# Unit 0's first product of the experts' layer in seven block products instead of eight

## The chip, the cores and the metric

The kernel runs on one core of a Trainium2 chip. The metric is device time in microseconds (us) of one execution; the median of several executions is compared. The profiled execution has a time of its own and a span (first to last instruction), and all times inside it are counted from the start of the span. An engine is named as in the profile: PE is TensorE (its weight loads are PEld), DVE is VectorE, ACT is ScalarE, POOL is GpSimd, SP is SyncE, which starts most transfers.

## The reference

Two stages. First attention over 8 batches, 8 heads, 576 positions and 64 features, with a band mask (half of the heads plain, half dilated by 4). Then a mixture of 8 experts over the 4608 rows of 512 features: each row takes an expert, or keeps that of the row before it, and passes through that expert's two layers.

```python
for b in range(B):
    prev_e = -1
    for s in range(S):
        fresh_e = int(np.argmax(logits[b, s]))
        if s == 0 or local_gate[b, s] < 0.5:
            e = fresh_e
        else:
            e = prev_e if prev_e >= 0 else fresh_e
        prev_e = e
        ...
        h = np.maximum(x[b, s] @ w1[e], 0.0)
        out[b, s] = p[e] * (h @ w2[e])
```

Everything is fp32. `w1[e]` is 512 x 1024, `w2[e]` 1024 x 512.

## The kernel before

**Attention** runs over 32 pairs of heads (n = 0 to 31), some 3.4 to 5 us each. In iteration n, TensorE makes the scores of pair n (L328, L334); VectorE masks half of them (L339) and ScalarE takes the exponential of both halves (L341). TensorE multiplies with the values of pair n - 1 (L387), and VectorE divides by the sums (L391, L392). GpSimd copies rows of V between blocks of the same pair (L279). Every second iteration TensorE turns rows of an earlier pair into columns (L408, L412), which ScalarE copies out (L409, L414); SP stores them in DRAM for later gathers.

**Routing** is done in four groups of 1152 rows. Each group is a chain of small steps: logits (L441, copied by L445), `fresh` (turned by L453, then ten small steps on VectorE, L455 to L476), `carry` (L484, L486, L488), `carry_over` (L494, L496 to L499), `carry_in` (L504, L505), `choose` (L510 to L524), `gate` (L532 to L538), `place` (L548, L549, L551), `lanes_of` (L557 to L564), four matrices (L575 twice, L585, L591) and their products (L600, added by L605). The second group ends the *early* routing, from which the tokens of units 0 and 1 are taken (L703 the expert numbers, L728 to L738 the token numbers); the fourth ends the *late* one (L617 and `count`, L620 to L691; L701, L703; L718, L722; L728 to L743), from which all other units come. The steps wait in a list (`waiting`). `gap(SHARE)` takes some of them twice in each iteration of attention, by their costs; afterwards `work_gap` takes one lot at each `yield` of a unit's products, and up to two entries of a second list, `soon`, which holds sums. So the order on TensorE, VectorE, GpSimd and SP is the order in which this code runs; ScalarE's alone is left to a scheduler.

**Units.** A unit is 256 rows of one expert (kinds `plain` and `pair`), or 128, 64 or 32. Its rows are gathered by GpSimd (L855, by `tok` and `pos`), turned by TensorE and copied by ScalarE (`features`, L870, L871). `hidden` makes the 1024 hidden values, `output` the product with the second weights. Units 0 and 1 are early, the rest late. A *pair* unit splits each product of 2 x 2 blocks into seven block products in place of eight (`chain`), with sums of blocks that VectorE makes beforehand: four of the first weights (`sums_left`, L818 to L821, into `sums[0]`), four of the tokens (`sums_right`, L824 to L827, into `xc`), the same again for the second product (`sums[1]`, `hc`). Of the first seven, ScalarE copies the first three out of PSUM (L955), VectorE adds three more (L961) and ScalarE applies the relu (L962, L959). A *plain* unit, and unit 0 is the only one, does all blocks: in `hidden` 32 matmuls 256 wide (L925), with a relu after each eight (L927), in `output` 16 matmuls 512 wide (L1011), scaled by L1015.

**Weights.** SP loads them (L781) into slots: a 2 MB load for each of a unit's two weights, skipped by a condition if the slot already holds the expert. Slot 0's first weights are loaded beforehand for expert 0, in four parts in iterations 11, 14, 17 and 20 (L312).

After the last pair of heads come the turning of unit 0's rows, that of the last attention rows, the logits of the last group, and then `run_hidden(0, [])`, `run_output(0, ...)`, `run_hidden(1, ...)`, `output(1)`; in the middle of the last, `feed` asks for the late units' weights and tokens. Unit 2's rows are turned (L870) before the last block product of unit 1's output.

Of the kernel before, what the change touches and what calls it, by code (L numbers as in the profile page):

```python
# [14 lines left out]
Act = mybir.ActivationFunctionType  # L15
# [7 lines left out]
P = 128  # L23
# [3 lines left out]
DK, FK = D // P, F // P  # L27
# [10 lines left out]
NPB = B * NP  # L38
# [179 lines left out]
def whole(ctx, tc, exact, bad, qk, v, wgl, w1, w2, con, adm, msk, qmk, out, cst, wg, ones, warm):  # L218
    nc = tc.nc
# [31 lines left out]
    def bank(shape, name):  # L251
        return banks.tile(shape, F32, name=name, tag="bank")
# [498 lines left out]
    for k in range(n_pairs):  # L751
        i = k // 2 + k % 2 * (n_pairs // 2)
        units.append(dict(kind="pair", col=2 * i, slot=k % 2, late=True))
        while len(others) > min(n_others, max(n_others * (n_pairs - 1 - k) // (n_pairs - 2), k < n_pairs - 1)):
            kind, col = others.pop(0)
# [3 lines left out]
    def of_unit(u, what, j=0, rows=P):  # L759
        return tiles[what, units[u]["late"]][:rows, units[u]["col"] + j:units[u]["col"] + j + 1]  # L760
# [6 lines left out]
    def weights(u, second):  # L767

        i = units[u]["slot"]
        loads.add((u, second))  # L770
        if not second:
            units[u]["held"] = holds.get(i)
            holds[i] = nc.values_load(of_unit(u, "experts", rows=1), engines=[ET.SP], min_val=0, max_val=E - 1,
                                      skip_runtime_bounds_check_because="clamped to the experts")
            units[u]["expert"] = holds[i]
        e, held = units[u]["expert"], units[u]["held"]
        w, s, pattern = (w2, raw2, "p m f -> p (m f)") if second else (w1, raw1, "p m k f -> p (m k f)")
        if second and not units[u]["late"] and isinstance(held, int):
            held = None
        more = {} if held is None else dict(cond=e != held, cond_hint=False)  # L780
        nc.sync.dma_start(out=s[i].rearrange(pattern), in_=w[bass.ds(e, 1)].rearrange("o p x -> (o p) x"), **more)  # L781
# [5 lines left out]
    def gap(add=None):  # L787
        if add is not None:
            credit[0] = min(credit[0] + add, add)
        alone = False  # L790
        while waiting and not alone and (add is None or credit[0] >= 0):
            f, cost, _ = waiting.pop(0)
            credit[0] -= cost
            if f:
                f()
            alone = add is None or not waiting or waiting[0][2]
# [7 lines left out]
    def now(push):  # L804
        for f in push:
            f()
# [22 lines left out]
    def sums_of_weights(u, second):  # L829

        i = units[u]["slot"]
        assert (u, second) in loads
        if second:
            return sums_right(sums[1], *(quarter(raw2[i], k, j, True) for k in range(2) for j in range(2)))
        return sums_left(sums[0], *(quarter(raw1[i], f, k, False) for f in range(2) for k in range(2)))
# [3 lines left out]
    def tiles_of(u):  # L839
        return 2 if units[u]["kind"] in ("pair", "plain") else 1  # L840

    def rows_in(u):
        return dict(half=ROW, few=FEW).get(units[u]["kind"], P)
# [18 lines left out]
    def features(u):  # L862
        kind = units[u]["kind"]
        rows = rows_in(u)
        xe[u] = mw.tile([P, DK, 2 * P], F32, name="xe")
        for j in range(tiles_of(u)):
            x = xg.pop((u, j)).rearrange("p g f -> p (g f)")
            tp = bank([P, DK, P], "tp")
            for kk in range(DK):
                nc.tensor.transpose(tp[:, kk, :rows], x[:rows, kk * P:(kk + 1) * P], ident[:rows, :rows])  # L870
            nc.scalar.copy(xe[u][:, :, j * P:j * P + rows], tp[:, :, :rows])  # L871
        if kind == "pair":
            xc[u] = mw.tile([P, 4, DK // 2, P], F32, name="xc", bufs=1)
            return sums_right(xc[u], *(xe[u][:, 2 * k:2 * k + 2, j * P:(j + 1) * P]
                                       for k in range(2) for j in range(2)))
        return []
# [27 lines left out]
    def hidden(u):  # L904
        i, kind = units[u]["slot"], units[u]["kind"]
        ht[u] = h = stage.tile([P, FK, 2 * P], F32, name="h", bufs=2)
        w, x = raw1[i], xe[u]
        if kind in ("half", "few"):
            rows = rows_in(u)
            parts = P // rows  # L910
            t = bank([P, F // parts], "hp")
            for kk in range(DK):
                for v in range(parts):
                    nc.tensor.matmul(t[v * rows:(v + 1) * rows], lhsT=x[:, kk, :rows],
                                     rhs=w[:, v * FK // parts:(v + 1) * FK // parts, kk], start=(kk == 0),
                                     stop=(kk == DK - 1), tile_position=(0, v * rows), skip_group_check=True)
                yield True
            nc.scalar.activation(h[:, 0:4 // parts].rearrange("p m t -> p (m t)"), t, Act.Relu)
            return
        if kind == "plain":  # L920
            for m in range(FK):
                if m % 2 == 0:
                    t = bank([P, 2, 2 * P], "hp")
                for kk in range(DK):
                    nc.tensor.matmul(t[:, m % 2], lhsT=w[:, m, kk], rhs=x[:, kk], start=(kk == 0), stop=(kk == DK - 1))  # L925
                if m % 2:
                    nc.scalar.activation(h[:, m - 1:m + 1], t, Act.Relu)  # L927
                yield True
            return
        if kind == "full":  # L930
            for m in range(FK):
                if m % (FK // 2) == 0:
                    t = bank([P, FK // 2, P], "hp")
                to = t[:, m % (FK // 2)]
                for kk in range(DK):
                    nc.tensor.matmul(to, lhsT=w[:, m, kk], rhs=x[:, kk, :P], start=(kk == 0), stop=(kk == DK - 1))
                if m % (FK // 2) == FK // 2 - 1:
                    v = m * 2 // FK
                    nc.scalar.activation(h[:, v * FK // 2:(v + 1) * FK // 2, :P],
                                         t, Act.Relu)  # L940
                yield True
            return
        xyz = [bank([P, FK // 2, P], "hp") for _ in range(3)]

        def at(k):
            return h[:, k // 2 * FK // 2:(k // 2 + 1) * FK // 2, k % 2 * P:(k % 2 + 1) * P]

        def product(to, a, b, first):
            for m in range(FK // 2):
                for kk in range(DK // 2):  # L950
                    nc.tensor.matmul(to[:, m], lhsT=a[:, m, kk], rhs=b[:, kk], start=first and m == 0 and kk == 0,  # L951
                                     stop=(kk == DK // 2 - 1), skip_group_check=True)

        def keep(k, of):
            nc.scalar.copy(at((0, 1, 3)[k]), of)  # L955

        def finish(k, of):
            if k == 2:
                nc.scalar.activation(at(2), of, Act.Relu)  # L959
            else:  # L960
                nc.vector.tensor_tensor(at(k), of, at(k), op=Alu.add)  # L961
                nc.scalar.activation(at(k), at(k), Act.Relu)  # L962

        yield from chain((lambda i_, k: quarter(w, i_, k, False), lambda s: sums[0][:, s]),
                         (lambda k, j: x[:, 2 * k:2 * k + 2, j * P:(j + 1) * P], lambda s: xc[u][:, s]),
                         *xyz, product, keep, finish)
        units[u]["sums"] = sums_left(hc, at(0), at(2), at(1), at(3))
# [86 lines left out]
                         *xyz, product, keep, finish)  # L1054


    pause, rows = (None, 0, True), []

    def route(g, slow):
        steps = [(logits, 0, True), (fresh, 3.0, True), (carry, 1.0, True), (carry_over, 0.5, True), (carry_in, 0.5, True),  # L1060
# [30 lines left out]

    def early_weights():
        weights(0, False)

    def late_tokens():
        tokens(True)
        gather(FIRST)

    for n in range(NPB + 2):
        if n < NPB:  # L1100
            (scores_exact if exact else scores)(n)
        for k in range(NPB)[n + 1 if n else 0:n + 2]:
            share(k)
        gap(SHARE)
        if 1 <= n <= NPB:
            values(n - 1)
        if n == NPB + 1:
            assert len(rows) <= 4
            now(features(0))
        if n >= 3 and n % 2 == 1:  # L1110
            turn((n - 3) // 2)
            if (n - 3) // 2 % (2 * GB) == 2 * GB - 1:
                route((n - 3) // 2 // (2 * GB), n == NPB + 1)
        gap(SHARE)
        if n + 3 < NPB:
            load(n + 3)
        if n >= 3 and n % 2 == 1:
            store((n - 3) // 2)
        if n in (11, 14, 17, 20):
            load_first(0, (n - 11) // 3)  # L1120
        if n == NPB + 1:
            weights(0, True)
            weights(1, False)
        if rows:
            if n <= NPB:
                paced(n - 1)
            rows.pop(0)()
# [161 lines left out]
```

## Time and profile before

| | us |
|---|---|
| three executions | 666.64, 667.72, 669.94 |
| their median | 667.72 |
| profiled execution | 663.76 |
| its span | 661.8 |
| PE busy in the span | 646.6 |
| DVE busy in the span | 372.5 |
| L925: TensorE busy, records | 15.1, 64 |
| L925: first start, last start | 152.3, 169.6 |

The granted TensorE clock was 1.00 throughout. A line of groups gives the kernel's line, engine, operation, what is written and read, the shape, how many; behind the bar the busy time in us and the mean ns of one; behind the next the time for which its engine was idle just before them, and what ended that. In a timeline a line begins with start and length in us, and the brackets give the idle time before it and what ended it. Neighbouring fp32 matmuls overlap in the records, so distances between starts tell more than lengths.

### The profile page before, as it was taken

The numbers are of one execution on the slowest core, as the hardware profiler recorded it, in microseconds if no ns is written. First come the engines' busy times: TensorE is split into PE (matmuls) and PEld (weight loads), VectorE is DVE, ScalarE is ACT, GpSimd is POOL, SyncE is SP. The second block draws the span as 40 slices with busy tenths as digits, with TensorE's granted clock in tenths as the row PEclk, the third lists the DMA queues.
The fourth block names the chain that finished last, engine by engine and source line by source line (L and its number), as shares of the span: only waits on it lengthen the run. The fifth ranks groups of instructions, "written<-read, shape, count | busy, mean of one in ns | idle before, by whom it ended". The sixth has DMA issues, their size and how long they took to land. (4 is left out here: it accounts for less than half of the span.)

```text
span 661.8 us, 15170 instructions
## 1 busy us (share of the span) xinstructions
PE 646.6 (98%) x6402; PEld 568.2 (86%) x6402; DVE 372.5 (56%) x755; ACT 188.7 (29%) x348; POOL 188.1 (28%) x169
## 2 busy tenths in 40 slices
PE   8999999999999999999999999999999999999996
PEld 6988888888588999999599989998899989899893
DVE  3558578683596595372537382727464536547441
ACT  3544343442112331222122222231222232223210
POOL 3322222242115420322552153223144113051011
PEclk9999999999999999999999999999999999999999
DMA  8999899749205398574533456541045451454001
GB/s 313 325 297 322 280 283 319 247 124 354 88 33 190 129 418 314 187 280 169 226 132 141 154 203 223 229 164 49 16 177 215 179 219 59 155 193 148 1 32 50
DMA packets 29356, 126.31 MB, mean 191 GB/s; under 512 B 4349, under 2 KB 13789, under 8 KB 25312
## 3 DMA queue, kind: packets, MB, share of 16 engines
q1 hardware_dynamic: 22480, 106.05, 44.4%
q0 software_dynamic: 6800, 19.21, 8.5%
q8 instruction: 52, 0.85, 0.5%
q14 instruction: 24, 0.20, 0.1%
HBM read 142.02 MB, written 19.20 MB: 244 GB/s over the span
## 5 line engine op out<-in xcount | busy, mean ns | idle before, releaser
L979 POOL DMA_INDIRECT out_dram<-y,tok x36 | 55.0, 1527 | 292.3 <-DVE y L1048 124.5
L951 PE MATMUL hp<-xc,sum 128*128 128x128 f32 x720 | 85.6, 275 | 0.4 <-DVE sum L818 0.4
L951 PEld LDWEIGHTS hp<-xc,sum 128*128 128x128 f32 x720 | 82.8, 192 | 0.8 <-PE hp L951 0.5
L1033 PE MATMUL yp<-sum,hc 128*128 128x256 f32 x360 | 82.6, 379 | 0.0
L961 DVE TENSOR_TENSOR h<-hp,h 128x512 f32<-128x512 f32 x45 | 30.9, 690 | 90.8 <-PE hp L951 90.1
L1033 PEld LDWEIGHTS yp<-sum,hc 128*128 128x128 f32 x360 | 68.3, 190 | 9.4
L1048 DVE SCALAR_TENSOR_TENSOR y<-yp,gate,y 128x256 f32<-128x256 f32 x45 | 21.7, 482 | 75.1 <-issue 48.1
L279 POOL COPY vt<-vt 32x1040 f32<-32x1040 f32 x32 | 34.0, 1065 | 94.2 <-DMA vt<-in_v_dram 63.0
L951 PE MATMUL hp<-xe,raw 128*128 128x128 f32 x480 | 58.8, 276 | 0.0
L951 PEld LDWEIGHTS hp<-xe,raw 128*128 128x128 f32 x480 | 56.6, 192 | 1.8 <-issue 1.5
L1033 PE MATMUL yp<-raw,h 128*128 128x256 f32 x240 | 57.0, 380 | 0.0
L334 PE MATMUL two<-kq 64*96 64x64 f32 x1152 | 54.5, 244 | 0.2 <-issue 0.2
L334 PEld LDWEIGHTS two<-kq 64*96 64x96 f32 x1152 | 53.7, 162 | 0.3 <-issue 0.3
L855 POOL DMA_INDIRECT xg<-xd,tok x40 | 45.5, 1138 | 27.3 <-PE hp L951 15.0
L1033 PEld LDWEIGHTS yp<-raw,h 128*128 128x128 f32 x240 | 44.4, 190 | 5.5
L955 ACT COPY h<-hp 128x512 f32<-128x512 f32 x45 | 26.4, 586 | 79.3 <-PE hp L951 75.3
L962 ACT ACTIVATE h<-h 128x512 f32<-128x512 f32 x45 | 28.3, 630 | 67.2 <-DVE h L961 67.2
L855 POOL DMA_INDIRECT xg<-xd,pos x40 | 44.1, 1102 | 11.8 <-issue 10.8
L339 DVE SCALAR_TENSOR_TENSOR pr<-two,mk 96x512 f32<-96x512 f32 x32 | 21.9, 685 | 43.8 <-ACT pr L341 32.3
L387 PE MATMUL pv<-vt,pr 96*64 96x65 f32 x1280 | 44.7, 224 | 1.0 <-POOL vt L279 1.0
L387 PEld LDWEIGHTS pv<-vt,pr 96*64 96x64 f32 x1280 | 40.2, 138 | 3.7 <-POOL vt L279 1.2
L1041 ACT ACTIVATE y<-yp,gate 128x256 f32<-128x256 f32 x45 | 21.2, 474 | 55.5 <-PE yp L1033 48.8
(223 smaller groups left out, 1004.6 us busy)
## 6 DMA issues: line engine op xcount, KB each, us to landing
raw<-in_w_dram SPq DMA_DIRECT2D x48, 2048.0 KB
kq<-in_qk_dram SPq DMA_DIRECT2D x32, 592.0 KB
vt<-in_v_dram SPq DMA_DIRECT2D x32, 292.5 KB
xd<-x SPq DMA_DIRECT2D x16, 512.0 KB
raw<-in_w_dram SPq DMA_DIRECT2D x4, 512.0 KB
xd<-x SPq DMA_DIRECT2D x16, 64.0 KB
xg<-xd,tok POOLq DMA_INDIRECT x40, 3.2
xg<-xd,pos POOLq DMA_INDIRECT x40, 3.4
```

The lines of the kernel that those rows point to most:

```text
L279: nc.gpsimd.tensor_copy(vt[:WIN, :, 1:], vt[QB:, :, :NB - 1])
L334: nc.tensor.matmul(sc[:KW, u, k * QB:(k + 1) * QB], lhsT=kt[h, i * QB:i * QB + KW], rhs=qt[h, i * QB:(i + 1) * QB], start=bool(late), stop ...
L339: nc.vector.scalar_tensor_tensor(pr, sc[:KW, :, :w], -CEIL, mk[:, kind].unsqueeze(1).to_broadcast([KW, 2, w]), Alu.max, Alu.min)
L387: nc.tensor.matmul(pv[h * QB:(h + 1) * QB, k - a, u], lhsT=pr[i][:, u], rhs=vt[:, u, i], start=True, stop=True, tile_position=(0, h * QB), ...
L855: nc.gpsimd.indirect_dma_start(out=x[:rows, g], out_offset=None, in_=xd[g] if units[u]["late"] else xd[g][:EARLY * GS], in_offset=bass.Ind ...
L951: nc.tensor.matmul(to[:, m], lhsT=a[:, m, kk], rhs=b[:, kk], start=first and m == 0 and kk == 0, stop=(kk == DK // 2 - 1), skip_group_chec ...
L955: nc.scalar.copy(at((0, 1, 3)[k]), of)
L961: nc.vector.tensor_tensor(at(k), of, at(k), op=Alu.add)
L962: nc.scalar.activation(at(k), at(k), Act.Relu)
L979: nc.gpsimd.indirect_dma_start(out=out, out_offset=bass.IndirectOffsetOnAxis(ap=of_unit(u, "tok", j), axis=0), in_=y, in_offset=None, boun ...
L1033: nc.tensor.matmul(to, lhsT=a[:, m], rhs=b[:, m], start=first and m == 0, stop=(m == FK // 2 - 1), skip_group_check=True)
L1048: nc.vector.scalar_tensor_tensor(at(k), of, of_unit(u, "gate", k // 2), at(k), Alu.mult, Alu.add)
```

## The change

Unit 0 keeps its kind `plain`, but its first product now goes through `chain` like a pair's: 56 matmuls 128 wide in place of 32 that are 256 wide. The branch for it is gone from `hidden`. Its output is as before. Four sums of tokens (`xc`) come out of `features(0)` and are made at once, in the last round of the attention loop. The four sums of the weights in slot 0 are put in a list `firsts` when the early routing is through, and one of them is made per pair of heads, behind the iteration's routing steps; what is left at the end is made before `features(0)`. `chain` yields seven times where the old branch yielded eight times, so `work_gap` runs once less in unit 0's first product.

```diff
-        if kind == "pair":
+        if kind in ("pair", "plain"):
             xc[u] = mw.tile([P, 4, DK // 2, P], F32, name="xc", bufs=1)
             return sums_right(xc[u], *(xe[u][:, 2 * k:2 * k + 2, j * P:(j + 1) * P]
                                        for k in range(2) for j in range(2)))
...
-            return
-        if kind == "plain":
-            for m in range(FK):
-                if m % 2 == 0:
-                    t = bank([P, 2, 2 * P], "hp")
-                for kk in range(DK):
-                    nc.tensor.matmul(t[:, m % 2], lhsT=w[:, m, kk], rhs=x[:, kk], start=(kk == 0), stop=(kk == DK - 1))
-                if m % 2:
-                    nc.scalar.activation(h[:, m - 1:m + 1], t, Act.Relu)
-                yield True
             return
...
-    pause, rows = (None, 0, True), []
+    pause, rows, firsts = (None, 0, True), [], []
...
     def early_weights():
         weights(0, False)
+        firsts.extend(sums_of_weights(0, False))
...
         if n == NPB + 1:
             assert len(rows) <= 4
+            now(firsts)
             now(features(0))
...
         gap(SHARE)
+        if firsts and n <= NPB:
+            firsts.pop(0)()
         if n + 3 < NPB:
             load(n + 3)
```

## The prediction

> **What bounds the kernel now.** The page first: which engine is full.
>
> ```profile
> PE 646.6 (98%) x6402; PEld 568.2 (86%) x6402; DVE 372.5 (56%) x755; ACT 188.7 (29%) x348; POOL 188.1 (28%) x169
> ```
>
> TensorE is busy for 98% of the span, so a us taken from its stream shortens the kernel, and a us that it waits lengthens it. Next the groups with shapes kept apart (count | busy, mean ns | idle before): the product replaced, its new form, the new sums.
>
> ```profile
> L951 PE MATMUL hp<-xc,sum 128*128 128x128 f32 x720 | 85.6, 275 | 0.4 <-DVE sum L818 0.4
> L818 DVE TENSOR_TENSOR sum<-raw 128x1024 f32<-128x1024 f32 x15 | 18.3, 1219 | 0.0
> L925 PE MATMUL hp<-xe,raw 128*128 128x256 f32 x64 | 15.1, 384 | 0.0
> ```
>
> A matmul in the program is two records. Third, VectorE's timeline (start us, length) where the sums go in.
>
> ```profile
> 129.85 0.69 DVE L339 SCALAR_TENSOR_TENSOR pr<-two,mk 96x512 f32<-96x512 f32 x1 [4.42 <-ACT pr L341]
> ...
> 133.79 0.68 DVE L339 SCALAR_TENSOR_TENSOR pr<-two,mk 96x512 f32<-96x512 f32 x1
> ...
> 138.26 0.69 DVE L339 SCALAR_TENSOR_TENSOR pr<-two,mk 96x512 f32<-96x512 f32 x1 [1.49 <-ACT pr L341]
> ...
> 141.61 0.69 DVE L339 SCALAR_TENSOR_TENSOR pr<-two,mk 96x512 f32<-96x512 f32 x1 [0.23 <-ACT pr L341]
> ...
> 148.78 0.56 DVE L392 TENSOR_TENSOR x<-pv,rec 128x384 f32<-128x384 f32 x1
> ...
> 151.78 0.85 DVE L591 TENSOR_TENSOR what<-is_it,gates 96x672 f32<-96x672 f32 x1
> ```
>
> The brackets are VectorE's idle time: cover for one sum at 129.85 and at 138.26, none at 133.79, hardly any at 141.61. From there to 152.63 it is never idle. Last, TensorE's timeline in the same stretch, and its weight loads later.
>
> ```profile
> 136.20 0.17 PE L494 MATMUL last<-cst,run 12*1 12x12 f32 x1
> ...
> 146.20 1.38 PE L387 MATMUL pv<-vt,pr 96*64 96x65 f32 x38 [1.03 <-POOL vt L279]
> ...
> 152.26 3.72 PE L925 MATMUL hp<-xe,raw 128*128 128x256 f32 x16
> 155.82 2.78 PE L600 MATMUL ap<-lane,what 96*112 96x128 f32 x24
> ```
>
> ```profile
> 211.28 0.20 PEld L870 LDWEIGHTS tp<-cst,xg 128*128 128x128 f32 x2 [0.30 <-DMA xg<-xd,tok]
> 211.64 0.20 PEld L870 LDWEIGHTS tp<-cst,xg 128*128 128x128 f32 x2 [0.16 <-DMA xg<-xd,pos]
> ```
>
> The stream has one hole before the product (1.03 us, for GpSimd's copy of V rows), and the first late gather already arrives too late for it.
>
> **What the Trainium skill says.** "VectorE: DVE Perf Modes", Why tensor_tensor can't do 2×_2P or 4×: two tensors take both read ports, so fp32 goes at one element per cycle. The trace agrees: 1219 ns for 1024. "TensorE: Matmul & The Clock Gate", Back-to-back issue gap: in a stream, weight load and matmul together set the spacing, so a narrower matmul isn't cheaper in proportion. Here that is slight: records follow each other at 0.112 us (128 wide, 1.79 us for 16) and 0.216 us (256 wide, 1.73 for 8). "SBUF — State Buffer", SBUF: two separate sides: VectorE with two SBUF inputs and GpSimd exclude each other. GpSimd's row store at L979 took 3.64 us at 179.49, beside VectorE's sums, and 1.01 at 186.30. The new sums can do this to its gathers.
>
> **The change, part by part.** All in the profiled execution: span 661.8, time 663.76, 3.96 below the median of 667.72. I add the shift to the median.
>
> *The product.* Before, 152.26 to 169.96 is 17.70; less what is queued in between (L600 2.62, L453 0.33, L484 0.09, L494 0.10, L504 0.12) 14.44 us. After, I take unit 1's seven products: 185.27 to 201.98 is 16.71, less L600 2.62, the wait and L701 0.44, L718 and L722 0.69: 12.96. That saves 1.48; by spacing, 64 x 0.216 - 112 x 0.112 = 1.28. I take 1.48.
>
> *The four sums.* 4 x 1.22 = 4.9 us of VectorE. The built order puts each just before an L339. Those before 129.85 and 138.26 lie in idle time (4.42, 1.49) and cost nothing; without that cover, 1.2 each. The one before 133.79 delays L486 and L488, for which TensorE's L494 waits, and the order shows two things more: ScalarE takes a later pair's Exp first, so the values product starts its second half some 0.4 late, and TensorE's second turning group now waits for ScalarE's copy of the first (0.59). I reckon L494 at 137.7, 1.5 late. The fourth starts at 142.9 (141.4 + 1.5), and its L339 at 144.0, 2.4 late. TensorE's delay then meets the hole at 146.20: the copy waited for hangs on gathers, not on VectorE. The last values product starts at 147.0, 0.8 late. But VectorE has no idle time: L392 of 148.78 ends at 151.6, not 149.34, and the turning of those rows (L408), which ran in 148.84 to 149.9, can only end at 151.9. L412 and L441 follow (2.4 us). The first product's bank, besides, now waits for ScalarE's copy of the logits (L445, 0.40 and 0.15 to reach it), which in the old order no product did. It starts at 154.9 instead of 152.26: 2.65 late. Bounds: 0 if all is absorbed; 3.4 if both uncovered sums, the Exp and the bank come through whole (2 x 1.22 + 0.4 + 0.55).
>
> *The sums of the tokens (xc).* Four at 0.37 apart, 1.5 us, ahead of L591. L591 ends at 151.78 + 0.85 + 2.2 + 1.5 = 156.3; TensorE comes to L600 after two products, 154.9 + 3.7 = 158.6. Nothing; with no cover, 1.5.
>
> *The draining.* Three adds at 0.69 on VectorE and three copies more on ScalarE. Queued behind each add are L486, L488 or L496 to L499; TensorE asks for them one product (1.85 us) later, and add, L486 and L488 sum to 1.3. Nothing; if that cover fails, 0.7 each.
>
> *One gap less.* Seven yields instead of eight: each routing step of the last group moves behind one more piece of TensorE's work. L510 falls into unit 0's product with its second weights (L1011). TensorE gets there 2.65 - 1.48 = 1.2 late, less 0.1 for L510. L548 stands behind six 512-wide matmuls, not four: 2 x 0.86 = 1.7. So L551 starts at 175.0 + 1.1 + 0.1 + 1.7 = 177.9, and from 175.0 to 205 VectorE has no idle time: 2.9 late, but for 0.3 that order gives back at the tokens' numbers (L728: 199.21 to 201.8, since one add and one sum change places with it). The gathers on GpSimd's queue start 2.6 later, and land at 213.9 and 214.25. TensorE arrives at L870 of unit 2 at 210.62 + 1.1 + 0.75 (hc's sums behind the late numbers) = 212.5, and waits: it leaves at 214.5 instead of 211.9, 2.6 late. If the gathers land faster than before, 1.7. No row shows which: I take the middle, 2.1. The expert numbers (L703) come at 201.2, not 197.5, so SP asks for unit 2's weights 3.7 later; they moved in 202 to 211 and are needed at 213.65 + 2.1 = 215.8: about 1 us to spare.
>
> *After that* every engine's order is the old one and TensorE is full, so the shift stays: **+2.1 us, 667.72 + 2.1 = 669.8**. A measurement of this kernel can tell about 0.5% (3.3 us) from no change, so I forecast no change that shows.
>
> **The rivals.**
> *The cover holds.* For: half the sums lie in idle time, and the hole at 146.20 can take 1 us. Then only the product is left, 667.72 - 1.5 = 666.2. Against: VectorE is busy without a gap from 141.6 to 152.6. In between (no delay early, the routing's gap kept) it is 2.65 less than my sum: 667.2.
> *The weights come late.* One mechanism on the slow side: SP's load of unit 2's first weights, 3.7 us later, shares the queues with gathers that are later too; the first product and L818 of unit 2 wait for it. For: DMA is 76 to 98% busy in 202 to 210. It decides from a landing after 215.8; 2.5 us past that gives 669.8 + 2.5 = 672.3, over 0.5% slower. Against: about 1 us of margin.
> *The change doesn't do what it says.* The first sum needs unit 0's weights, whose conditional load stands on SP's queue at 122.99. Had it moved 2 MB, the sum would hold up VectorE for some 5 us. Against: in 118 to 131 that queue moved 3.54 MB, what keys, values and rows make up; it was skipped.
>
> **How the numbers follow.** My forecast 0.58, mostly within 0.5%; the cover holds, wholly or in part, 0.22; weights late 0.16; a gain over 3.3 us from something not seen 0.04. Faster by over 0.5%: 0.05 (this, and a run's scatter); slower: 0.17 (weights late, and the end of my bounds); the same: 0.78. The range reaches from 666.0 (cover holds) to 672.2 (the early delay at its bound and the gathers at theirs give 669.8 + 0.75 + 0.5 = 671.1; the rest is for the weights' case).
>
> **What would show it.** The first product starts near 154.9 and takes 13.0 us of TensorE without what lies between; VectorE runs without a gap from 142.9; the wait for GpSimd's copy at 146.2 is gone; L870 of unit 2 waits 1 to 2 us for its gather; L701 falls behind the fifth product. I am wrong if the first product starts before 153.5, or if unit 2 starts earlier than 213.6.

## The result, and the profile after

Fourteen executions of each kernel: 671.14 us after, 669.39 before (medians); ratio 1.0022, 95% interval 1.0002 to 1.0042, so +1.5 us, between +0.1 and +2.8. The ratio, here and below, leaves out executions over 1.5% above the fastest of their kernel, one of each here. The kernel is slower, but by less than the 0.5% that the forecast took for a change that shows. The profiled execution after took 668.86 us (span 667.1), 5.1 more than the one before. About 3 of those 5.1 are there at unit 2; the rest comes behind 408 us, most of it in a gap that the traces of kernels with and without the change show (e12 below).

The engines' line of the page after, and one line of its groups with shapes kept apart:

```profile
PE 647.1 (97%) x6450; PEld 569.1 (85%) x6450; DVE 380.4 (57%) x766; ACT 190.8 (29%) x351; POOL 191.1 (29%) x169
```

```profile
L941 PE MATMUL hp<-xe,raw 128*128 128x128 f32 x512 | 62.7, 276 | 1.1 <-ACT le L445 1.1
```

The group of the old product (L925, 15.1 us) is gone, VectorE has 7.9 us more. The product's matmuls (L951 before) are L941 now. The 1.1 us behind L941 are a wait that the kernel before didn't have. VectorE's timeline in the stretch of the sums (L819 to L821 are the second to fourth):

```profile
129.92 0.69 DVE L339 SCALAR_TENSOR_TENSOR pr<-two,mk 96x512 f32<-96x512 f32 x1 [3.05 <-PE two L334]
...
133.86 1.86 DVE L819 TENSOR_TENSOR sum<-sum,raw 128x1024 f32<-128x1024 f32 x1
135.65 0.67 DVE L339 SCALAR_TENSOR_TENSOR pr<-two,mk 96x512 f32<-96x512 f32 x1
...
138.30 1.19 DVE L820 TENSOR_TENSOR sum<-raw 128x1024 f32<-128x1024 f32 x1
139.85 0.69 DVE L339 SCALAR_TENSOR_TENSOR pr<-two,mk 96x512 f32<-96x512 f32 x1 [0.36 <-ACT pr L341]
...
143.75 1.20 DVE L821 TENSOR_TENSOR sum<-raw,sum 128x1024 f32<-128x1024 f32 x1
144.87 0.68 DVE L339 SCALAR_TENSOR_TENSOR pr<-two,mk 96x512 f32<-96x512 f32 x1
...
155.95 0.84 DVE L591 TENSOR_TENSOR what<-is_it,gates 96x672 f32<-96x672 f32 x1
```

The first and the third sum left idle time ahead of their L339 (3.05, 0.36): they lay in cover. The second and the fourth have none, and the last L339 stands at 144.87 instead of 141.61. TensorE in the same stretch:

```profile
137.80 0.17 PE L494 MATMUL last<-cst,run 12*1 12x12 f32 x1 [0.41 <-ACT xt L409]
...
146.73 0.34 PE L412 MATMUL tp<-cst,x 64*128 64x64 f32 x2 [1.31 <-ACT xt L409]
...
152.19 0.44 PE L408 MATMUL tp<-cst,x 128*128 128x128 f32 x2 [0.20 <-DVE x L392]
...
156.11 2.05 PE L941 MATMUL hp<-xe,raw 128*128 128x128 f32 x16 [1.14 <-ACT le L445]
...
206.78 3.72 PE L1023 MATMUL yp<-sum,hc 128*128 128x256 f32 x16 [0.40 <-DVE hc L818]
```

The waits name ScalarE (L409, L445) more often than VectorE. The hole of 1.03 us at 146.20 is gone, and the first product starts 3.85 us late (156.11, before 152.26). Unit 2's second gather, for which TensorE's weight loads waited before:

```profile
214.65 0.20 PEld L870 LDWEIGHTS tp<-cst,xg 128*128 128x128 f32 x2 [0.18 <-issue]
```

No gather holds it up now. What held up the stream is at 206.78: VectorE's sum of hidden values for unit 1's output.

### The profile page after: what moved, and what is told of

Same layout as the page of the kernel before. It is cut to its first block, busy times and chain, and to the rows that moved or that the text cites. A ratio compares the mean times of both kernels' runs of the same rounds, so it can differ in the third digit from the quotient of the medians.

```text
span 667.1 us, 15283 instructions
## 1 busy us (share of the span) xinstructions
PE 647.1 (97%) x6450; PEld 569.1 (85%) x6450; DVE 380.4 (57%) x766; ACT 190.8 (29%) x351; POOL 191.1 (29%) x169
## 5 line engine op out<-in xcount | busy, mean ns | idle before, releaser
L969 POOL DMA_INDIRECT out_dram<-y,tok x36 | 57.0, 1584 | 291.6 <-DVE y L1038 119.7
L941 PE MATMUL hp<-xc,sum 128*128 128x128 f32 x768 | 91.7, 275 | 0.4 <-DVE sum L818 0.4
L941 PEld LDWEIGHTS hp<-xc,sum 128*128 128x128 f32 x768 | 88.6, 192 | 0.7 <-PE hp L941 0.5
L951 DVE TENSOR_TENSOR h<-hp,h 128x512 f32<-128x512 f32 x48 | 32.9, 690 | 92.1 <-PE hp L941 81.5
L941 PEld LDWEIGHTS hp<-xe,raw 128*128 128x128 f32 x512 | 60.4, 192 | 4.0 <-issue 2.0
L941 PE MATMUL hp<-xe,raw 128*128 128x128 f32 x512 | 62.7, 276 | 1.1 <-ACT le L445 1.1
L855 POOL DMA_INDIRECT xg<-xd,tok x40 | 46.9, 1174 | 26.7 <-PE hp L941 13.5
L945 ACT COPY h<-hp 128x512 f32<-128x512 f32 x48 | 28.1, 585 | 86.2 <-PE hp L941 81.4
L952 ACT ACTIVATE h<-h 128x512 f32<-128x512 f32 x48 | 30.2, 630 | 68.4 <-DVE h L951 60.0
L339 DVE SCALAR_TENSOR_TENSOR pr<-two,mk 96x512 f32<-96x512 f32 x32 | 21.9, 684 | 40.8 <-ACT pr L341 27.6
```

The lines of the kernel that those rows point to most:

```text
L339: nc.vector.scalar_tensor_tensor(pr, sc[:KW, :, :w], -CEIL, mk[:, kind].unsqueeze(1).to_broadcast([KW, 2, w]), Alu.max, Alu.min)
L855: nc.gpsimd.indirect_dma_start(out=x[:rows, g], out_offset=None, in_=xd[g] if units[u]["late"] else xd[g][:EARLY * GS], in_offset=bass.Ind ...
L969: nc.gpsimd.indirect_dma_start(out=out, out_offset=bass.IndirectOffsetOnAxis(ap=of_unit(u, "tok", j), axis=0), in_=y, in_offset=None, boun ...
```

## The experiments

All ratios are to the kernel before, run in between on the same chip; "changed kernel" is the one after. There were three rounds, each on another chip: e1 to e4, e5 to e8, e9 to e12. To read traces of executions that differ before the change begins, I count from pair 28's L339 (129.85 before, 129.92 after). In half of the traces TensorE's granted clock was cut somewhere between 138 and 158 us (to 0.50 at its lowest), in the kernel before too; there the place of the first product can't be read, and the table leaves it out.

| kernel | ratio, 95% interval | L339 of pair 28 to first product | first product to unit 1's turning | that to unit 2's |
|---|---|---|---|---|
| before | | 22.41 | 17.84 | 40.52 |
| changed | 1.0022 (1.0002 to 1.0042) | 26.19 | 16.18 | 41.50 |
| e1 sums only | 1.0035 (1.0018 to 1.0053) | | 17.84 | 40.52 |
| e2 product only | 0.9988 (0.9970 to 1.0006) | | 16.18 | 41.50 |
| e3 sums in cover | 0.9976 (0.9956 to 0.9996) | 23.83 | 16.18 | 41.50 |
| e4 other bank | 1.0000 (0.9973 to 1.0027) | | 16.18 | 41.50 |
| e5 changed again | 0.9994 (0.9959 to 1.0029) | 25.58 | 16.18 | 41.49 |
| e6 ScalarE's order | 1.0002 (0.9970 to 1.0035) | 24.34 | 16.18 | 41.49 |
| e7 gap back | 0.9983 (0.9955 to 1.0010) | | 16.52 | 40.52 |
| e8 cover, order, gap | 0.9973 (0.9950 to 0.9995) | | 16.52 | 40.53 |
| e9 before, order | 1.0002 (0.9983 to 1.0021) | | 17.85 | 40.52 |
| e10 as e8 | 0.9987 (0.9967 to 1.0007) | 23.16 | 16.52 | 40.52 |
| e11 cover, order | 0.9961 (0.9938 to 0.9983) | 22.91 | 16.18 | 41.49 |
| e12 before again | | | 17.84 | 40.53 |

The two right-hand columns repeat to 0.01 us or so in every kernel with the same work there. The third, from the undisturbed traces alone, differs by 0.6 between the two traces of the changed kernel.

**e1, the sums alone.** The old branch for the product and `features` without token sums are put back into the changed kernel:

```diff
-        if kind in ("pair", "plain"):
+        if kind == "pair":
             xc[u] = mw.tile([P, 4, DK // 2, P], F32, name="xc", bufs=1)
...
+        if kind == "plain":
+            for m in range(FK):
...
+            return
```

> The changed kernel with the old eight-block product of unit 0 put back: the four sums of its weights are still made at their four places, and nothing reads them; no sums of tokens. Theory (the sums and what they push are the cost): the first product starts where it does in the changed kernel, at 156.1 us and not at 152.3; nothing is saved by the product, the eighth gap is there, so the shift of 3.8 goes on: unit 2's first turning (L870) near 214.4 instead of 210.6, time 3.5 to 4 us over the kernel before. Rival (the missing gap costs most): the first product starts at 156 too, but unit 2 starts at 211.6 or earlier, and the time is within 1 us of before.

Measured: 1.0035, +2.3 us (1.2 to 3.5), less than expected but slower beyond doubt. From the first product on everything is as in the kernel before (17.84 and 40.52), so all of it arises ahead of the product. The rival with the missing gap falls: this kernel has all eight.

**e2, the product alone.**

```diff
-        firsts.extend(sums_of_weights(0, False))
...
+    nc.vector.memset(sums[0], 0.0)
```

> The changed kernel without the four sums of unit 0's weights: their tile is filled with zeros once at the start, so the seven products run on the right shapes with a wrong operand. The sums of the tokens and the seven gaps stay. Theory: the first product starts as before, at 152.3, takes 12.9 us of TensorE instead of 14.4, so unit 1's turning is at 168.6 instead of 170.1; the routing that lies one gap later gives some back, as gathers then come later than TensorE: unit 2's first turning at 209.6 to 210.6 instead of 210.6, time 0 to 1 us under before. Rival (the missing gap is the cost of the change): unit 2 at 212 or later. Rival (the sums of tokens are not hidden): the first product or L600 starts over 1 us late.

Measured: 0.9988, -0.8 us (-2.0 to +0.4), where 0 to -1 was expected. (This kernel leaves out the four sums; its product reads zeros in their place.) The clock was cut (0.57 in 138 to 146), so the start of the product can't be judged. From there to unit 1's turning it saves 1.66 us, and gives 0.98 back up to unit 2's. The tokens' sums are hidden: L600 follows the first product by 3.67 us without a wait, as in the changed kernel. e1 and e2 add up to +1.5, the result of the whole change: sums and product are its two halves. Each is known to some 1.2 us only, so a term of that size that they have in common would not show.

**e3, the sums in cover.**

```diff
-        if firsts and n <= NPB:
-            firsts.pop(0)()
+        for _ in range({27: 3, 29: 1}.get(n, 0)):
+            firsts.pop(0)()
```

> The changed kernel with the four weight sums at other places: three one after the other where VectorE had 4.42 us of idle time (ahead of the L339 that was at 129.85), the fourth where it had 1.49 (ahead of the L339 at 138.26). Nothing is left out. Theory (the place makes the cost): the last turning and the first product start within 0.7 us of before, at 152.3 to 153.0, there is no wait for ScalarE's copy of the logits ahead of it, and unit 2 starts at 209.8 to 211.0, time 0 to 1 us under before. Rival (VectorE is full later anyway, so any 4.9 us of work comes out at the end of attention): the first product starts at 155 or later, as in the changed kernel.

Measured: 0.9976, -1.6 us (-2.9 to -0.3). The same 4.9 us of work cost 1.4 us ahead of the product (23.83 against 22.41), not 3.8 or 3.2 as in the two traces of the changed kernel, so the rival falls. But the place isn't all of this gain. Here the product follows the last logits (L441) by 2.08 us, without the wait for L445, where the changed kernel took 3.29; that alone is 1.2, and why the wait is gone the traces don't tell. The 1.4 is also more than the 0.7 I had allowed, and unit 2 is still 0.7 late (81.51 us behind L339, before 80.77). A candidate for what is left lay in ScalarE's timeline of this kernel, and just so of the changed one (`pr<-two` is a pair's first exponential, `pr<-pr` its second). The changed kernel:

```profile
129.23 0.70 ACT L341 ACTIVATE pr<-two 96x640 f32<-96x640 f32 x1 [0.74 <-PE two L334]
132.78 0.70 ACT L341 ACTIVATE pr<-two 96x640 f32<-96x640 f32 x1 [2.85 <-PE two L334]
133.38 0.62 ACT L341 ACTIVATE pr<-pr 96x512 f32<-96x512 f32 x1
```

ScalarE sits idle for 2.85 us waiting for pair 29's scores, and only then makes pair 28's second exponential, whose input was ready at 130.6 (L339, 129.92 + 0.69). In the kernel before it ran there:

```profile
130.57 0.63 ACT L341 ACTIVATE pr<-pr 96x512 f32<-96x512 f32 x1 [0.71 <-DVE pr L339]
```

ScalarE alone is ordered by a scheduler. With sums ahead of L339 it chose the other order in all of the changed kernel's traces, in e1, e3, e4 and e7. Whether that costs anything, e6 and e11 show.

**e4, another bank for the last logits.** In the changed kernel unit 0's first product waits for the copy of the last logits (L445), as it would if both lay in one PSUM bank; in the kernel before it doesn't wait. Here the logits are put elsewhere.

```diff
-        lp = bank([P, NQ], "lp")
+        lp = bank([P, NQ], "lp") if g < NG - 1 else twos.tile([P, 2, 512], F32, name="two")[:, 0, :NQ]
```

> The changed kernel with the last group's logits written to a PSUM bank that unit 0's first product doesn't use (a bank of the scores, which are done by then). Nothing is left out. Theory (the wait for ScalarE's copy of the logits is a term of its own): the first product starts at 155.0 to 155.3 instead of 156.1 without a wait for L445, and some of that reaches unit 2: 212.8 to 213.5 instead of 213.8; time 0.3 to 1 us under the changed kernel. Rival (the wait only shows TensorE's own end of L441, which the records put too early): the first product starts at 155.8 or later.

Measured: 1.0000 (0.9973 to 1.0027). The product starts straight behind the logits, and L445 only after it has begun (157.61 against 157.48): the wait is gone. But the clock was cut during L441, which took 3.77 us instead of 2.08, and the time's interval is too wide. Inconclusive on the price; e6 gives it.

**e5, the changed kernel again**, beside the next three.

> The changed kernel again, beside the next three on one chip, so that their differences to it are measured there. Every theory expects what it did before: 1 to 2 us over the kernel before, the first product some 3.5 to 4 us later than in the kernel before.

Measured: 0.9994 (0.9959 to 1.0029), -0.4 us, lower than the first time with an interval that holds both. In the trace the first product is 3.2 us later than in the kernel before (25.58), under the 3.5 expected: here the second sum took 1.21 us and not 1.86.

**e6, ScalarE's order by hand.**

```diff
-    ctx.enter_context(tc.manual_schedule(engines={ET.PE, ET.DVE, ET.Pool, ET.SP}))
+    ctx.enter_context(tc.manual_schedule(engines={ET.PE, ET.DVE, ET.Pool, ET.SP, ET.Activation}))
```

> The changed kernel with ScalarE's order written by hand too, like that of the other engines: in attention it is then that of the kernel before (a pair's second exponential ahead of the next pair's first). The sums stay where they are. The last logits also come to lie in another PSUM bank than unit 0's first product, so it doesn't wait for their copy. Nothing is left out. Theory (VectorE's added work is most of the cost, ScalarE's order and the bank some 1 to 1.5 of it): the first product at 154.5 to 155.2 us instead of 156.1, time 0.7 to 1.5 us under the changed kernel. Rival (ScalarE's order is the main cost, VectorE's sums are mostly absorbed): the first product at 153.5 or earlier, time at least 2 us under the changed kernel. Rival (order and bank don't matter): no earlier than 155.8.

Measured: 1.0002 (0.9970 to 1.0035), so the time doesn't tell it from e5. The trace does. ScalarE:

```profile
130.14 0.70 ACT L341 ACTIVATE pr<-two 96x640 f32<-96x640 f32 x1 [0.74 <-PE two L334]
131.55 0.63 ACT L341 ACTIVATE pr<-pr 96x512 f32<-96x512 f32 x1 [0.71 <-issue]
133.84 0.68 ACT L341 ACTIVATE pr<-two 96x640 f32<-96x640 f32 x1
136.62 0.63 ACT L341 ACTIVATE pr<-pr 96x512 f32<-96x512 f32 x1 [2.10 <-DVE pr L339]
```

TensorE in the kernel before (its first product at 152.26 follows), in e5 and in e6:

```profile
150.18 2.15 PE L441 MATMUL lp<-xt,wg 128*32 128x288 f32 x32
...
158.81 2.15 PE L441 MATMUL lp<-xt,wg 128*32 128x288 f32 x32
162.16 2.05 PE L941 MATMUL hp<-xe,raw 128*128 128x128 f32 x16 [1.20 <-ACT le L445]
...
153.10 2.15 PE L441 MATMUL lp<-xt,wg 128*32 128x288 f32 x32
155.17 2.05 PE L941 MATMUL hp<-xe,raw 128*128 128x128 f32 x16
```

The product follows the logits by 2.07 us as in the kernel before (2.08), where e5 took 3.35 and the changed kernel's first trace 3.29: the bank's wait cost 1.2 to 1.3. The order by itself bought nothing: the logits start 22.27 us after pair 28's L339 here, and 22.23 in e5 with the scheduler's order. (The first trace has 22.90, but there the second sum took 1.86 us, against 1.21 in e5 and 1.22 here; that is the 0.6, and its cause is below.) The fourth of ScalarE's lines shows a reason: with a sum ahead of pair 29's L339, that pair's second exponential has to wait for VectorE, whatever the order. The first product is 24.34 us behind L339, 1.2 earlier than in e5, so the gain is of the size that the first theory had for order and bank, all of it the bank's. It is still 1.9 later than in the kernel before.

**e7, the eighth gap back.**

```diff
+    work_gap()
     run_hidden(0, [])
```

> The changed kernel with one routing gap more, ahead of unit 0's first product, so that the last group's steps lie as many gaps in as in the kernel before; the pause that this gap takes first meant nothing there. Nothing is left out. In the kernels with seven gaps unit 2 lost 0.9 to 1.0 us between unit 1's turning and its own, against the kernel with eight. Theory (the missing gap costs some 0.8 us): that loss is gone, unit 2's first turning at 212.8 to 213.2 instead of 213.8, time 0.5 to 1 us under the changed kernel. Rival (that loss has another cause, or the gathers set it): unit 2 at 213.6 or later, the time the same.

Measured: 0.9983 (0.9955 to 1.0010), not to be told from e5. In the trace unit 1's turning to unit 2's takes 40.52 again instead of 41.49, as the theory has it; 0.34 of it is paid back before unit 1's turning, where L510 lies again and L600 lies one product earlier. VectorE's wait at the hidden values' sums (0.40) is gone with it.

**e8 and e10, all put together; e11, without the gap; e9 and e12, controls.** e8 and e10 are one kernel: e3's places, e6's order, e7's gap. e11 leaves `work_gap()` out, e9 has ScalarE's order alone on the kernel before, e12 is the kernel before.

> All that was found put together: the weight sums three and one in VectorE's idle time, ScalarE's order written by hand, the eighth gap back. Nothing is left out. Theory (then only the product's saving of 1.5 us is left): the first product starts within 0.5 us of the kernel before, counted from the scores of pair 28, unit 2 1.0 to 1.5 us earlier than there, time 1.0 to 1.6 us under the kernel before. Rival (something later takes the gain, or VectorE is late anyway): the time no better than with the sums moved alone, 0.8 us under before.

> The combination again (sums three and one in idle time, ScalarE's order by hand, the eighth gap), for a trace in which TensorE's clock is not cut between 146 and 156 us, and a second measure of its time. Counted from pair 28's L339, the kernel before has its first product at 22.4 us and unit 2's first turning at 80.8, the changed kernel at 26.2 and 83.9. Theory: 22.3 to 22.9 and 79.3 to 79.8, time 1.0 to 1.8 us under the kernel before. Rival (a rest of the sums' cost remains): first product at 23.4 or later, unit 2 at 80.3 or later, time less than 0.8 us under before.

> That combination without the eighth gap. Theory (the gap is worth 0.8 us at unit 2, and it stays): first product as in the combination, unit 2's first turning 0.7 to 1.0 us later than there, time 0.4 to 1.0 us longer than there. Rival (what the gap gains is taken back later): the time the same within 0.3.

> Control: the kernel before with ScalarE's order written by hand, as in the last two experiments; in attention that is the order it had. Nothing is left out. Theory: the time within 0.7 us of the kernel before, and first product and unit 2 as there. Rival (the hand-written order helps by itself, in the later units): 1 us or more under before; then part of the gain of those experiments isn't the change's.

> The kernel before once more with a profile, to see how much the places used as landmarks move between executions: counted from pair 28's L339, first product at 22.2 to 22.7 us, unit 2's first turning at 80.5 to 81.1, if they are good to a few tenths. If they are off by a us or more, differences of that size between traces prove nothing.

Measured: e8 0.9973 (-1.8 us, -3.3 to -0.3), e10 0.9987 (-0.9, -2.2 to +0.5), e11 0.9961 (-2.6, -4.1 to -1.1), e9 1.0002 (+0.1, -1.1 to +1.4). So nothing shows that the order by itself helps the kernel before. e11 has the lowest ratio of all, with an interval that overlaps those of e3, e8 and e10 and of the changed kernel's second measure (0.9994), not that of its first (1.0022). VectorE in e11, then TensorE:

```profile
126.14 1.22 DVE L818 TENSOR_TENSOR sum<-raw 128x1024 f32<-128x1024 f32 x1
127.38 1.23 DVE L819 TENSOR_TENSOR sum<-sum,raw 128x1024 f32<-128x1024 f32 x1
128.53 1.22 DVE L820 TENSOR_TENSOR sum<-raw 128x1024 f32<-128x1024 f32 x1
130.40 0.69 DVE L339 SCALAR_TENSOR_TENSOR pr<-two,mk 96x512 f32<-96x512 f32 x1 [0.66 <-ACT pr L341]
...
137.35 1.19 DVE L821 TENSOR_TENSOR sum<-raw,sum 128x1024 f32<-128x1024 f32 x1
138.91 0.69 DVE L339 SCALAR_TENSOR_TENSOR pr<-two,mk 96x512 f32<-96x512 f32 x1 [0.37 <-ACT pr L341]
```

```profile
149.89 1.15 PE L408 MATMUL tp<-cst,x 128*128 128x128 f32 x8 [1.51 <-ACT xe L871]
151.23 2.15 PE L441 MATMUL lp<-xt,wg 128*32 128x288 f32 x32
153.31 2.05 PE L941 MATMUL hp<-xe,raw 128*128 128x128 f32 x16
```

All four sums leave idle time ahead of their L339, and the first product comes 22.91 us behind pair 28's, 0.5 later than in the kernel before (1.51 of waiting for ScalarE's copy of unit 0's rows has come in, where 1.03 for GpSimd's and 0.24 for ScalarE's went out). e10 has it at 23.16, over the 22.9 expected. Its unit 2 is at 80.20 (79.3 to 79.8 expected): of the 1.3 us that the product and the gap save from there on, 0.6 is left. It lies between the theory and its rival.

Place and order can now be told apart. This is the start of the last logits behind pair 28's L339 in the undisturbed traces (us; the kernel before has 20.33), ahead of the bank's wait:

| | sums one per pair | sums in idle time |
|---|---|---|
| scheduler's order | 22.23 (e5), 22.90 (first trace) | 21.75 (e3) |
| order by hand | 22.27 (e6) | 20.83 (e11), 21.08 (e10) |

The place alone gains 0.5 against e5, the order alone nothing, both together 1.1 to 1.4: the order counts (0.7 to 0.9) only once no sum delays the L339 that the second exponential waits for. Each number is one trace, and e10 and e11, which are the same up to here, lie 0.25 apart.

The gap's worth stays open. In the traces it saves 0.63 from the first product to unit 2 (57.04 against 57.67), but directly behind it e10 loses 0.39: unit 2's turning to the next product takes 1.50 us instead of 1.11, with 0.30 of idling in the middle, for which the trace names no cause (late rows would look so). e11's unit 2 is 0.4 behind e10's, where 0.7 to 1.0 was expected, and one unit on nothing of it is left: unit 3's first turning is 96.53 us behind pair 28's L339 in both (96.91 in the kernel before), as e11's rival had it. And the times go the other way (e11 under e10 and e8), with intervals that overlap. Nothing here shows a gain by the gap in the time.

e12's clock was cut in the very stretch, so it says nothing on how far the front part moves between executions of the kernel before; one undisturbed trace of it is all there is. It tells something else. TensorE in e12, in the first small unit (L993, that is L983 in the changed kernel):

```profile
413.95 1.17 PE L993 MATMUL yp<-raw,h 128*32 128x128 f32 x33
415.50 0.31 PE L993 MATMUL yp<-raw,h 128*32 128x128 f32 x2 [0.38 <-issue]
416.22 0.29 PE L993 MATMUL yp<-raw,h 128*32 128x128 f32 x1 [0.41 <-issue]
416.91 1.08 PE L993 MATMUL yp<-raw,h 128*32 128x128 f32 x28 [0.40 <-issue]
```

These 64 records take 1.95 us in a row in the kernel before's first trace, 4.04 here, and 3.56 in the changed kernel's first trace. So the gaps, which have no visible cause, cost the kernel before 2.1 us in e12 and the changed kernel 1.6. They are not the change's, and are most of the last 2.1 us between the two profiled executions; about 3 were there at unit 2. None of the four traces of the first round has them, all eight of the other two rounds do (1.6 to 2.3 us), so they seem to go with the chip or the time rather than with the kernel.

## Why the prediction held, step by step

The forecast was +2.1, the time says +1.5 (0.1 to 2.8): the right size, made of terms some of which were wrong. In part that is luck. The sum was made in terms of the profiled execution, and there the shift at unit 2 is 3.1 and 2.5 us.

*The product: right.* 16.18 us from the first product to unit 1's turning, less 3.26 for the same steps queued in between, is 12.92 us; 12.96 was predicted. With L510 no longer in there, the stretch is 1.66 shorter.

*The four sums: right in kind, 1.1 us too small.* The first product is 3.78 us late by pair 28's L339 (3.17 in e5), not 2.65, and the first trace is over my upper bound of 3.4. L494 came at 137.80 (137.7 predicted), free sums were free, the hole at 146.20 was used up. What the lateness is made of, counted from e5 by way of e6 and e11:

- the bank: "0.55" was 1.3 (3.35 against 2.07 between L441 and the product). In e1 and e7, with the same wait, it was 0.6: there ScalarE's copy starts 2.2 us behind the start of L441, in the changed kernel's two traces 2.8 and 2.9, for which they name no reason.
- ScalarE's order by itself: 0.4 and part of a 0.59 wait were in the sum; taking the order back moved the logits by nothing (22.23 to 22.27).
- VectorE's place, with the order right: 1.4 (24.34 to 22.91).
- 0.5 is left (22.91 to 22.41) even with the sums covered.

That is the 3.2 of e5; it has to add up, as each term is the distance to the next kernel in the row. The first trace has 0.6 more, from one sum that met GpSimd. The split is made from one trace of each kernel, and e10, built like e11 but for the gap, differs from it by 0.25.

The prediction priced each sum at 1.22. The second took 1.86 in the changed kernel's first trace, and beside the fourth it was GpSimd that stood still. GpSimd's timeline there:

```profile
133.60 1.04 POOL L279 COPY vt<-vt 32x1040 f32<-32x1040 f32 x1 [2.63 <-PE rp L484]
...
143.67 2.19 POOL L279 COPY vt<-vt 32x1040 f32<-32x1040 f32 x1 [1.90 <-PE two L334]
```

The second sum began inside the first of these copies, and took 0.64 longer. The second copy is 1.15 over its usual 1.04, about the length of the sum (its record starts 0.08 ahead of the sum's, but it was the copy that stood). I had cited the Trainium skill ("SBUF — State Buffer", SBUF: two separate sides) for GpSimd's gathers only; what it says, that the two exclude each other and the one that comes second blocks, holds for any GpSimd instruction that reads SBUF, and these copies of V run once per pair just there. The first meeting agrees with that; in the second the records have the order the other way round. In e5 the second sum took 1.21 and in e7 1.86 again: whether they meet is chance, and the 0.6 between the two traces of the changed kernel goes with it.

*The tokens' sums and the draining: right.* L591 is done at 156.79 (156.3 predicted), TensorE comes to L600 at 159.78; no product waits for an add.

*One gap less: the amount right by luck, the cause wrong.* I had 0.93 of it at unit 2 (2.1 less 1.17). From unit 1's turning to unit 2's it costs 0.98; counted from the first product on, and so without what L510's move shifts between the two stretches, 0.63 (57.67 against 57.04). But I put it on the gathers: TensorE comes to L870 of unit 2 "and waits: it leaves at 214.5 instead of 211.9". There was no such wait; gathers issued 3.8 us later (204.86, before 201.10) landed in time. It was the 0.75 in my sum, "hc's sums behind the late numbers", that became a wait on VectorE (0.40 at 206.78), and everything that I added for gathers beyond that wasn't there. Only with the gap back, in e10, do the rows seem to bind.

*Afterwards: right.* The shift is 3.2 at unit 2's turning (213.79 against 210.62) and stays at 3.0 from unit 3's to 408 us.

*Trace and time.* At unit 2 the traces have the changed kernel 3.1 and 2.5 us late, the time has 1.5 and, in e5, -0.4 with a wide interval. e3 (0.7 late in the trace, 1.6 early in time) and e11 (0.2 and 2.6 early) go the same way. The trace before was a lucky one as a whole (663.76, under each of the 14 timed executions), and I had no second one with TensorE's full clock. Part of the scatter in time is the clock. Among executions with a mean clock of 0.997 or more, the medians differ from the kernel before by +0.9 us in e5 (6 against 15 executions), +2.6 in e1, -0.5 in e2, -0.8 in e3 and -1.9 in e11. That brings e3 and e5 nearer to their traces, but it was picked afterwards and has no interval. The rest isn't settled.

*The rivals.* "The cover holds" was the wrong name for what could have been had: it didn't hold where the sums stood, but does hold where idle time is (e3, e11). "The weights come late": no wait at unit 2's first product. "It doesn't do what it says": the first sum ran at 125.66 without a wait for its load. Of the signs that the prediction named, the wait at unit 2's L870 didn't come, and the first product came 1.2 us later than named.

## What to carry to other kernels

Put added work where the timeline of its engine shows idle time, and not evenly: the same four sums made the first product 3.2 to 3.8 us late one per pair, and 0.5 to 0.8 three and one with the order kept. After any edit on one engine, look at what the edit does to the order and the buffers that are chosen on the others: 1.2 to 1.3 us of that was a bank's wait that the edit brought by accident, and moving the sums paid in full only with ScalarE's order put right as well. Compare with a second trace of the same kernel before a difference of half a us is given a cause. Price a saving and its preparation apart (here -0.8 and +2.3): the sum of them hides that one is worth keeping.

## What the runs showed of the hardware that was not expected

- In seven of fourteen traces TensorE's granted clock was cut between 138 and 158 us, whatever the kernel: e1 had 0.50 in 146 to 150 us with TensorE busy for all of it. Its profiled execution took 674.84 us at a mean clock of 0.985, where its median is 667.75; over the executions of the kernel before in the three rounds (67, 51 and 59), the mean clock goes along with 73 to 83% of the variance of the time.
- VectorE's two-input sums and GpSimd's copies in SBUF hold each other up: a sum went from 1.22 to 1.86 us, a copy from 1.04 to 2.19. In two traces of one kernel (first trace, e5) the sum met the copy once and once not.
- Idle time of TensorE without a visible cause, 1.6 to 2.3 us in all, at the first 32-row unit: in none of the four traces of the first round and in all eight of the other two. The kernel before hadn't it in its first trace and had it in e12.
